# Conditioning rows of a fused state-space and SwiGLU block: four of six computed in four column parts of the matrix engine, the branch gate multiplied into K's column sums, a new order of loads and tasks

## The chip, the cores and the metric

The kernel runs on one core of one Trainium2 chip. A core has five instruction queues: PE (TensorE, matrix products), DVE (VectorE), ACT (ScalarE), POOL (GpSimd) and SP (SyncE, which here only issues transfers). Each queue takes its instructions strictly in program order; an instruction that waits for another engine or for a transfer holds those behind it. The metric is the device time of one launch in microseconds. Before the change it is 489.13 us, the median of 3 runs (488.37 to 490.04).

## The reference, cut to what matters

L = 2048 tokens, D = 448 channels, N = 256 states, F = 1792 hidden features, all in float32.

```python
mod = (silu(c) @ w_mod).reshape(1, 6, 1, D)      # c: 1 x 448, w_mod: 448 x 2688
sa, ca, ga, sb, cb, gb = mod[:, 0], ..., mod[:, 5]
h = layernorm(x) * (1 + ca) + sa
x = x + ga * (causal_conv(h, K) + h * Dskip)     # K from A, B, C, log_dt: 448 x 2048
h = layernorm(x) * (1 + cb) + sb
x = x + gb * ((silu(h @ w_gate) * (h @ w_up)) @ w_down)
```

The rows are numbered as in w_mod: 0 is the shift sa, 1 the scale ca, 2 the branch gate ga, 3 the shift sb, 4 the scale cb, 5 the gate gb of the end.

## The kernel before

The 2048 tokens are 16 tiles of 128, taken in blocks of 2, 2, 3, 3, 3 and 3 tiles. For each block a loop runs over 14 feature tiles f of 128 hidden features: `gate_up(f)` (L686) makes the gate and up products on PE with weights split into a rounded high and a low part, ScalarE takes the Silu, VectorE multiplies, ScalarE rounds the product (phi) and VectorE takes the low part (plo), and `down(f - 1)` (L739) adds the product of the feature tile before into one bank per token tile. Between these, the convolution part of the next block's tiles is done in steps.

Two paths exist for the convolution. A flag, computed on the chip from the size of dt * A, picks the short one with these inputs: K(l) is taken as m0 + l * m1 for every channel, so the convolution becomes products with a triangular matrix of ones (`tri`), a ramp and a running row (`run0`, `run1`) carried from tile to tile. m0 and m1 are sums over the states: `total` (L345, on ScalarE) and `slope` (L382, on VectorE). They come as columns (channels on partitions, four chunks of 128, the last with 64 channels twice) and are turned into a row, the same on all partitions, by `row_of` (L350): a matmul per chunk with the identity.

The change lies in the first 40 us, before block 0's feature loop. That stretch prepares everything: it loads x, the six state matrices (`sa` to `sf`, 448 KB each), w_mod's six groups (two loads each, 448 and 336 KB) and the first weights; computes the six rows, m0 and m1; does the convolution part of token tiles 0 and 1; normalises them, turns them to channels on partitions (`to_channels`) and splits them into high and low parts (`high`, `low`). Block 0's first feature tiles need the split weights w0, w1, w2 (`split_w`: ScalarE rounds, another engine takes the low part) and d0, d1 (`split_d`).

The order is written out by hand in two strings. `ORDER` (L41) gives SyncE's first loads. `PLAN` (L43) names tasks of the dictionary `todo`; each task issues its instructions on its engine when its name comes, so PLAN sets the order on every queue. Names: `pa`, `ps`, `pg`, `cb`, `sb` and `e` are the two halves of a row (1, 0, 2, 4, 3, 5); `S1` to `S3`, `a2`, `a3` the state sums; `k0`, `k1` the sums as rows; `o..` the products of tiles 0 and 1; `l0`, `l1` the left-over sums of these tiles for `run0` and `run1`, `lc` their copies; `tr`, `hi`, `lo` the turn to channels and the split; `x0`, `x1` the copies of the tiles out of their banks.

A row is computed by `mod_part` (L233): silu(c) as a stationary operand, repeated over 128 columns, against w_mod, so that the row comes out the same on all 128 partitions:

```python
pe.matmul(ps[:, 0:D], cs[:, k:k + 1].to_broadcast([128, 128]), w[:, k * D:(k + 1) * D],
          start=k == 0, stop=False)
```

Chunks 0 to 2 are summed in the bank; chunk 3 comes as two matmuls of 224 columns. The gate ga multiplies k0 and k1 as rows in their banks (`gm0`, `gm1` on VectorE) and the row of Dskip (`gd` on GpSimd), which was spread by a matmul at the start. The shift sb is added as a row after the normalisation (`norm_2`), and its columns `sbc`, for later blocks, come from four transposes (`cols`). The end gate is copied from its bank (`eg`) to `gb`, which is first used when block 0 ends (L808).

The flag is read into registers on every engine (L486) and a branch follows; then block 0 starts with gate_up(0), whose first bank is DN[2], and whose first instruction on ScalarE is the Silu (L718).

Of the kernel before, what the change touches and what calls it, by code (L numbers as in the profile page):

```python
# [40 lines left out]
ORDER = """sf x0 x1 sc m10 se m11 sd m20 m21 m00 sb m01 sa m40 m41 d0 w0 m30 m31 m50 w2 d1 x2 w1 x3 d2 m51"""  # L41

PLAN = """t1 t4 pa0 t2 pa1 pg0 pg1 t3 S1 ca h00 S2 ps0 wr wi ps1 a2 m0 t5 a3 sq1 k0 cb0 S3 ga cb1 w0 h01 gd h11 m1 k1 gm0 h10  # L43
hd0 sb0 gm1 hd1 gc1 v00 v10 gc0 o00 o01 sq0 o02 o10 v01 sa w02 d10 o13 st0 r0 o12 cbr v11 d11 o11 o14 sb1 n10 w2 w01
st1 r1 d00 sbr e0 n11 n20 du0 tr0 n21 hi0 du1 tr1 l0 fs l1 sbt lo00 hi1 w1 lo10 fl lo01 sbc x1 e1 lo11 w11 w21 x0 eg
w22 lc w12 d01"""
# [11 lines left out]
def tile_kernel(ctx, tc, x, a_re, a_im, b_re, b_im, c_re, c_im, log_dt, dskip,  # L58
# [172 lines left out]
    cs = const.tile([128, 5], F32)  # L231

# [11 lines left out]
    def end_gate(ks):  # L244

        mod_part(CV, m5.rearrange("p a b -> p (a b)"), ks)
# [9 lines left out]
    with tc.tile_pool(name="pre", bufs=1) as pre:  # L256
        vec = pre.tile([128, 8], F32)
        sc.dma_start(vec, vecs)
        drow = pre.tile([1, D], F32)
        sc.dma_start(drow, dskip.rearrange("(o d) -> o d", o=1))  # L260
# [36 lines left out]
        ve.memset(cs, 0.0)  # L297

# [25 lines left out]
        pe.matmul(pd, all1[0:1, :], drow, start=True, stop=True)  # L324
        sc.copy(gd, pd)
# [11 lines left out]
                               (("h", F32, D), ("v0", F32, D), ("v1", F32R, D), ("hd", F32, D), ("h2", F32, 512)))  # L337
        sbr = pre.tile([128, 512], F32)
        ga = pre.tile([128, D], F32)
        t_, WV = f32(tri), po  # L340
# [4 lines left out]
        def total(o, t, scale):  # L345
            for k in range(4):
                a = part(t, k)
                sc.activation(sca[:, 0:a.shape[1]], a, AF.Copy, scale=scale[:, k:k + 1], accum_out=o[:, k:k + 1])

        def row_of(m, ps):  # L350

            for k in range(4):
                n = 128 if k < 3 else 64
                pe.matmul(ps[:, k * 128:k * 128 + n], m[:, k:k + 1].to_broadcast([128, 128]), ident if k < 3 else ident2,
                          start=True, stop=True)
            return ps[:, 0:D]
# [9 lines left out]
        def row_sbuf(to, g, bias, ends=((0, 0, D),)):  # L366
            for a, o, n in ends:
                sc.activation(to[:, o:o + n], psm[g][:, a:a + n], AF.Identity, bias=bias)

        def cols():  # L370
            psm["c"] = bank()
            for k in range(4):
                pe.transpose(psm["c"][:, k * 128:(k + 1) * 128], sbr[:, k * 128:(k + 1) * 128], ident)

        def cols_sbuf():
            sc.copy(sbc, psm["c"].rearrange("p (k c) -> p k c", k=4)[:, :, 0])

        def gate_row():
            sc.copy(ga, psm[2][:, 0:D])  # L379
            sc.dma_start(gad, ga[0:1])  # L380
# [7 lines left out]
        def left_over(ks):  # L388
            if 0 in ks:
                psm["l"] = bank()  # L390
            for k in ks:
                u, w = ((f32(left[:, 0]), v0[k]) if k < 2 else (left[:, k - 1], v1[k - 2]))
                pe.matmul(psm["l"][0:33, 0:D], u, w, start=k == 0, stop=k == 3)  # L393

        def left_sbuf():
            for z, r in enumerate((run0, run1)):
                sc.copy(r[0:1], psm["l"][32 * z:32 * z + 1, 0:D])

        def to_channels(q):
            for k in range(4):  # L400
                if q == 0:
                    pk[k] = bank()
                pe.transpose(pk[k][:, q * 128:q * 128 + 128], h2[q][:, k * 128:(k + 1) * 128], ident)

        def high(q):
            for k in range(4):
                c_ = slice(q * 128, (q + 1) * 128)
                sc.copy(hhi[:, k, c_], pk[k][:, c_])

        def low(q, ks):  # L410
            for k in ks:
                c_ = slice(q * 128, (q + 1) * 128)
                ve.tensor_tensor(hlo[:, k, c_], pk[k][:, c_], f32(hhi[:, k, c_]), op=OP.subtract)

        def norm_1(q):
            ve.scalar_tensor_tensor(h2[q][:, 0:D], os[q], n2.of[q][0], cbw, op0=OP.subtract, op1=OP.mult)

        def norm_2(q):
            ve.scalar_tensor_tensor(h2[q][:, 0:D], h2[q][:, 0:D], n2.of[q][1], sbr[:, 0:D], op0=OP.mult, op1=OP.add)
# [4 lines left out]
        def flag_sum():  # L424
            psm["z"] = bank()
            pe.matmul(psm["z"][0:1, 0:2], ones, sz, start=True, stop=True)

        def flag_of():
            zm = pre.tile([1, 1], F32)
            ve.tensor_reduce(zm, psm["z"][0:1, 0:2], axis=AX.X, op=OP.add)  # L430
            ve.tensor_scalar(flag, zm, SMALL * SMALL, None, op0=OP.is_le)

        pk = {}
# [10 lines left out]
            "S1": do(total, m0_, t1, dt), "S2": do(total, m0, t2, ndt), "S3": do(total, a1, t4, dt2),  # L444
            "a2": do(slope, (0, 1)), "a3": do(slope, (2, 3)),
            "m0": add(m0, m0, m0_), "m1": add(m1, a1, a2), "k0": do(row_of, m0, CV), "k1": do(row_of, m1, DN[2]),

            **{f"{n}{z}": do(row, g, z) for n, g in (("pa", 1), ("ps", 0), ("pg", 2), ("cb", 4), ("sb", 3)) for z in range(2)},
            "ca": lambda: sc.activation(ca1, psm[1][:, 0:D], AF.Identity, bias=1.0),
            "sa": copy(sa, lambda: psm[0][:, 0:D]), "ga": gate_row,  # L450
# [593 lines left out]
```

## Time and profile before

| | |
|---|---|
| three runs | 488.37, 489.13, 490.04 us |
| the profiled execution | 488.68 us, its span 486.9 us |
| mean granted clock of PE | 0.998 |
| busy: PE, weight loads, VectorE, ScalarE, GpSimd | 98%, 92%, 58%, 32%, 13% |
| moved | 31.24 MB, mean 64 GB/s; 310, 415 and 161 GB/s in the first three fortieths (12.2 us each) |
| first matmul of block 0 | 38.64 us |

The span runs from the first to the last instruction; the execution has 1.8 us around it. In the profile a line of the timeline gives a group of like instructions: the start in us, the time from its first start to its last end, the engine (PEld is PE's weight load, ACTq and SPq are transfers being issued), the kernel's line, what is written and read, and the count; in brackets the idle time of that engine just before and what ended it. An f32 matmul shows as two records on PE. Ends of matmuls are modelled and overlap the next start, so the pace is read from the starts.

### The profile page before, as it was taken

The page shows a single profiled execution, that of the slowest core. Times are in us where ns is not written, and L with a number is a line of the kernel's source. Part 1 is how long each engine was busy: PE and PEld are TensorE (multiplying, and loading weights), DVE is VectorE, ACT ScalarE, POOL GpSimd, SP SyncE. Part 2 cuts the span into 40 slices and gives each one's busy share as a digit, 9 for nine tenths or more (in the row PEclk, how much of TensorE's full clock was granted, in tenths as well). Part 3 has the DMA queues.
Part 4 walks back from the last instruction along what each step waited for, and adds up shares of the span by engine and source line. Part 5 has one row for each costly group of instructions (what it writes and reads, how often), then busy time and mean ns, then how long its engine had stood idle before and what let it go on. Part 6 is the DMA issues. An engine that isn't in the chain of part 4 may idle for free.

```text
span 486.9 us, 6980 instructions
## 1 busy us (share of the span) xinstructions
PE 477.3 (98%) x2725; PEld 447.4 (92%) x2725; DVE 283.2 (58%) x543; ACT 155.0 (32%) x338; POOL 61.8 (13%) x86
## 2 busy tenths in 40 slices
PE   8999999999999999999999999999999999999994
PEld 5749988999998999999999999999999999999994
DVE  4868999568886446574644667375475643222134
ACT  5665455522225112332312223231223222221111
POOL 2241001000000040410023221002241000000000
PEclk9999999999999999999999999999999999999999
DMA  8945762020000200101210011130001112000001
GB/s 310 415 161 156 235 193 88 15 96 1 0 3 14 83 1 0 42 30 52 80 44 0 2 43 45 43 114 0 2 0 45 43 44 75 23 1 0 1 0 63
DMA packets 18751, 31.24 MB, mean 64 GB/s; under 512 B 2578, under 2 KB 13460, under 8 KB 18708
## 3 DMA queue, kind: packets, MB, share of 16 engines
q1 hardware_dynamic: 18000, 30.52, 18.3%
q8 instruction: 23, 0.38, 0.3%
q10 hardware_dynamic: 708, 0.19, 0.2%
q14 instruction: 20, 0.16, 0.1%
HBM read 24.61 MB, written 6.03 MB: 63 GB/s over the span
## 4 chain that ended last, share of the span: by engine, by line
PE 94%; DVE 2%; ACT 2%; issue 1%; POOL 0%; DVEq 0%; POOLq 0%; ACTq 0%
PE bank L703 57%; PE dn L747 27%; PE bank L237 2%; PE bank L253 1%; PE dn L437 1%; PE bank L241 1%; ACT raw L196 1%; PE bank L907 1%; PE cv L908 1%; PE cv L906 1%; PE cv L237 0%; PE bank L393 0%; DVE raw L194 0%; PE bank L207 0%; PE bank L920 0%
## 5 line engine op out<-in xcount | busy, mean ns | idle before, releaser
L703 PE MATMUL bank<-hhi,gu 128*128 128x384 f32 (+1 forms) x1169 | 209.4, 318 | 0.0
L703 PEld LDWEIGHTS bank<-hhi,gu 128*128 128x128 f32 x1169 | 189.8, 188 | 3.2 <-issue 0.7
L703 PE MATMUL bank<-hlo,gu 128*128 128x384 f32 (+1 forms) x668 | 130.8, 317 | 0.0
L703 PEld LDWEIGHTS bank<-hlo,gu 128*128 128x128 f32 x668 | 109.2, 188 | 0.0
L731 DVE TENSOR_TENSOR bank<-raw,bank 128x384 f32<-128x384 f32 (+1 forms) x69 | 36.8, 534 | 122.7 <-PE bank L703 120.3
L734 ACT CAST phi<-bank 128x384 fp32r<-128x384 f32 (+1 forms) x83 | 36.9, 445 | 140.8 <-DVE bank L731 140.8
L718 ACT ACTIVATE raw<-bank 128x384 f32<-128x384 f32 (+1 forms) x70 | 32.9, 470 | 121.8 <-PE bank L703 115.3
L735 DVE TENSOR_TENSOR plo<-bank,phi 128x384 fp32r<-128x384 f32 (+1 forms) x83 | 42.5, 512 | 37.6 <-ACT phi L734 37.6
L747 PE MATMUL dn<-wdh,plo 128*128 128x448 f32 x218 | 58.0, 367 | 0.0
L747 PE MATMUL dn<-wdh,phi 128*128 128x448 f32 x218 | 58.0, 367 | 0.0
L747 PE MATMUL dn<-wdl,phi 128*128 128x448 f32 x218 | 57.6, 365 | 0.0
L747 PEld LDWEIGHTS dn<-wdh,plo 128*128 128x128 f32 x218 | 41.0, 188 | 3.6
L747 PEld LDWEIGHTS dn<-wdl,phi 128*128 128x128 f32 x218 | 41.0, 188 | 3.5
L747 PEld LDWEIGHTS dn<-wdh,phi 128*128 128x128 f32 x218 | 38.7, 188 | 1.8 <-ACT run L930 0.7
L168 POOL TENSOR_SCALAR rsb<-mvb 128x1 f32<-128x1 f32 (+2 forms) x13 | 4.7, 360 | 170.6 <-DVE mvb L152 170.6
L168 POOL TENSOR_SCALAR rsa<-mva 128x3 f32<-128x3 f32 (+1 forms) x6 | 1.4, 233 | 118.1 <-DVE mva L152 118.1
L124 ACT CAST gu<-raw 128x1024 fp32r<-128x1024 f32 x14 | 14.6, 1046 | 0.3 <-ACT ga L379 0.3
L881 POOL TENSOR_TENSOR m<-m,gm 128x448 f32<-128x448 f32 x9 | 10.4, 1152 | 21.3 <-DVE m L185 21.3
L895 DVE TENSOR_TENSOR vl<-m,vh 128x448 fp32r<-128x448 f32 x12 | 9.1, 755 | 6.7 <-ACT vh L894 6.1
L237 PE MATMUL bank<-wm,cs 128*128 128x448 f32 x30 | 12.5, 546 | 0.0
L126 DVE TENSOR_TENSOR gu<-raw,gu 128x768 fp32r<-128x768 f32 x13 | 12.3, 950 | 0.0
L118 DVE TENSOR_TENSOR wdl<-rawd,wdh 128x448 fp32r<-128x448 f32 x16 | 9.9, 621 | 3.4 <-ACT wdh L116 3.2
(213 smaller groups left out, 417.8 us busy)
## 6 DMA issues: line engine op xcount, KB each, us to landing
raw<-in_B_w_gate_up_dram SPq DMA_DIRECT2D x14, 512.0 KB, 3.8
rawd<-in_B_w_down_dram SPq DMA_DIRECT2D x16, 224.0 KB, 3.9
x<-in_A_u_dram SPq DMA_DIRECT2D x12, 224.0 KB, 2.9
out_dram<-x SPq DMA_DIRECT2D x11, 224.0 KB, 2.4
xd<-raw SPq DMA_DIRECT2D x9, 256.0 KB, 2.0
raw<-xd SPq DMA_DIRECT2D x36, 64.0 KB, 2.0
wm<-in_w_mod_groups_dram SPq DMA_DIRECT2D x5, 448.0 KB, 8.0
wm<-in_w_mod_groups_dram SPq DMA_DIRECT2D x5, 336.0 KB, 7.9
```

What stands on the lines that cost most here:

```text
L118: ve.tensor_tensor(lo, wdn[j], f32(hi), op=OP.subtract)
L124: sc.copy(wgu[j][:, :, 0:4, :], w)
L126: en.tensor_tensor(lo, w[:, :, 0:3, :], f32(hi), op=OP.subtract)
L237: pe.matmul(ps[:, 0:D], cs[:, k:k + 1].to_broadcast([128, 128]), w[:, k * D:(k + 1) * D], start=k == 0, stop=False)
L703: pe.matmul(ps[s][:, 0:n], w[:, s, a], (hlo if lo else hhi)[:, k, 0:n], start=first and q == 0, stop=end and q == len(ka) - 1)
L718: sc.activation(p[:, 0:n], ps[0][:, 0:n], AF.Silu)
L731: ve.tensor_tensor(ps[1][:, 0:n], p[:, 0:n], ps[1][:, 0:n], op=OP.mult)
L734: sc.copy(hi[:, 0:n], ps[1][:, 0:n])
L735: ve.tensor_tensor(lo[:, 0:n], ps[1][:, 0:n], f32(hi[:, 0:n]), op=OP.subtract)
L747: pe.matmul(dn[q][:, 0:D], u[:, cs], v, start=f == 0 and z == 0, stop=f == (NF - 3 if last else NF - 1) and z == 2)
L881: (ve if on_v else po).tensor_tensor(v, h, g, op=OP.mult)
L895: ve.tensor_tensor(vl, v0, f32(vh), op=OP.subtract)
```

## The change

Rows 2, 3, 4 and 5 are computed by a new function, `mod_quads`: each chunk k of 128 channels has its own 32 columns of the array and its own 32 partitions of the bank, so that four partial sums of the row stand in partitions 0, 32, 64 and 96. ScalarE copies the bank (`gpc`, `cpc`, `spc`, `gqc`). A vector `pick` with ones in partitions 0, 32, 64 and 96 then adds the four: for rows 2, 3 and 5 with the copy as stationary operand, which gives the sum as columns (`columns`: `gt`, `sbt`, `gbt`; five matmuls of one moving column each), for row 4 with `pick` as stationary operand, which gives it as a row (`ck`).

The gate ga, now as columns `gac`, multiplies m0, m1 and Dskip while these are columns of 4 elements; `gm0` and `gm1` fall away. Dskip comes with the small first load and is turned into a row by four matmuls (`gdr`). The shift sb is not added after the normalisation but with the split: `high` adds `sbc` on ScalarE, `low` on VectorE, with two chunks in one bank. The end gate goes as columns to DRAM and from there, repeated on all partitions, into `gb`; ScalarE issues these three transfers. The left-over sum for `run0` takes v0 of both tiles, added by GpSimd (`v0s`). w0's low part moves from GpSimd to VectorE. ORDER and PLAN are new: w_mod's groups come ahead of most weights.

```diff
-ORDER = """sf x0 x1 sc m10 se m11 sd m20 m21 m00 sb m01 sa m40 m41 d0 w0 m30 m31 m50 w2 d1 x2 w1 x3 d2 m51"""
+ORDER = """sf x0 x1 sc m10 se sd m11 m20 m21 m00 sb m01 sa m40 m41 m30 m31 w0 m50 m51 d0 w1 d1 x2 w2 x3 d2"""
...
-st1 r1 d00 sbr e0 n11 n20 du0 tr0 n21 hi0 du1 tr1 l0 fs l1 sbt lo00 hi1 w1 lo10 fl lo01 sbc x1 e1 lo11 w11 w21 x0 eg
+w01 spc v0s gq w02 fs tr0 sbt xn1 fl sbc gqc hi0 l0 lo0 tr1 l1 hi1 gbt lo1 gbc x0 x1 w1 d00 w11 w12 lc d01 w2 w21 w22 d10 d11"""
...
-    def end_gate(ks):
-
-        mod_part(CV, m5.rearrange("p a b -> p (a b)"), ks)
+    def mod_quads(ps, w):
+
+        for k in range(3):
+            pe.matmul(ps[32 * k:32 * k + 32, 0:D], cs[:, k:k + 1].to_broadcast([128, 32]), w[:, k * D:(k + 1) * D],
+                      start=True, stop=True)
+        for z in range(2):
+            pe.matmul(ps[96:128, z * D // 2:(z + 1) * D // 2], cs[:, 3 + z:4 + z].to_broadcast([128, 32]), w[:, 3 * D:NM],
+                      start=z == 0, stop=z == 1)
+
+    def chunks(t, k):
+
+        if k < 3:
+            return [(slice(0, 128), t[:, k * 128:(k + 1) * 128])]
+        return [(slice(64 * z, 64 * z + 64), t[:, 384:D]) for z in range(2)]
+
+    def to_dram(row, col):
+
+        sc.dma_start(row[:, 0:384].rearrange("o (k p) -> p (o k)", p=128), col[:, 0:3])
+        sc.dma_start(row[:, 384:D].rearrange("o p -> p o"), col[0:64, 3:4])
...
-        pd = bank()[:, 0:D]
-        pe.matmul(pd, all1[0:1, :], drow, start=True, stop=True)
-        sc.copy(gd, pd)
...
-        t_, WV = f32(tri), po
+        t_, WV = f32(tri), ve
...
+        def columns(n):
+
+            for k in range(4):
+                for e, t in chunks(qt[n], k):
+                    pe.matmul(psm[n][e, 448 + k:449 + k], t, pick, start=True, stop=True)
+
+        def spread_row():
+            pe.matmul(psm["c"][:, 0:D], pick.to_broadcast([128, 128]), qt["c"], start=True, stop=True)
+
+        def gd_row():
+            psm["d"] = bank()
+            row_of(gdm, psm["d"], ident[:, 0:64])
+
+        def end_gate():
+            sc.copy(gbc, psm["b"][:, 448:452])
+            to_dram(gbd, gbc)
+            sc.dma_start(gb, gbd.to_broadcast([128, D]))
+
+        def scaled(o, a, b):
+            po.tensor_tensor(o, a, b, op=OP.add)
+            po.tensor_tensor(o, o, gac, op=OP.mult)
+
+        def slope_of():
+            ve.tensor_tensor(m1, a1, a2, op=OP.add)
+            ve.tensor_tensor(m1, m1, gac, op=OP.mult)
...
-        def left_over(ks):
-            if 0 in ks:
-                psm["l"] = bank()
-            for k in ks:
-                u, w = ((f32(left[:, 0]), v0[k]) if k < 2 else (left[:, k - 1], v1[k - 2]))
-                pe.matmul(psm["l"][0:33, 0:D], u, w, start=k == 0, stop=k == 3)
+        def left_over(z):
+            if z:
+                for k in range(2):
+                    pe.matmul(CV[0:33, 0:D], left[:, 1 + k], v1[k], start=False, stop=k == 1)
+            else:
+                pe.matmul(CV[0:33, 0:D], f32(left[:, 0]), v0s, start=True, stop=False)
...
                 if q == 0:
-                    pk[k] = bank()
-                pe.transpose(pk[k][:, q * 128:q * 128 + 128], h2[q][:, k * 128:(k + 1) * 128], ident)
+                    pk[k] = pk[k - 1][:, 256:512] if k % 2 else bank()
+                o = pk[k][:, q * 128:q * 128 + 128]
+                if k < 3:
+                    pe.transpose(o, h2[q][:, k * 128:(k + 1) * 128], ident)
+                else:
+                    for e, t in chunks(h2[q], k):
+                        pe.matmul(o[e], t, ident, start=True, stop=True)
...
-                sc.copy(hhi[:, k, c_], pk[k][:, c_])
+                sc.activation(hhi[:, k, c_], pk[k][:, c_], AF.Identity, bias=sbc[:, k:k + 1])
...
         def flag_sum():
-            psm["z"] = bank()
-            pe.matmul(psm["z"][0:1, 0:2], ones, sz, start=True, stop=True)
+            pe.matmul(psm["s"][0:1, 460:462], ones, sz, start=True, stop=True)
```

How the queues change at the places that matter: first ScalarE's queue at the end of the stretch, before. The names: `hhi` is the rounded high part, `gu_158` is w1, `cv` holds the end gate's row, `dn_68` and `dn_69` are the banks of tiles 0 and 1, `p` is the Silu of gate_up(0).

```order
L408 CAST hhi<-bank 128x128 [waits PE_49] x2
L124 CAST gu_158<-raw 128x2x512 [waits DMAHW3_49]
L376 COPY sbc<-bank 128x4 [waits PE_49]
L473 COPY x_73<-dn_69 128x448 [waits DMAHW4_49]
L473 COPY x_72<-dn_68 128x448
L438 COPY gb<-cv 128x448 [waits PE_49]
L397 COPY run<-bank 1x448 x2
L486 TENSOR_LOAD flag [waits DVE_49]
L975 COMPARE_AND_BRANCH
L718 ACTIVATE p<-dn_70 128x256 [waits PE_49]
```

And after the change, from the end gate's columns `gbc` on; here w1 is `gu_154`, w2 `gu_160`, and `wdh_151` and `wdh_156` are d0 and d1:

```order
L400 COPY gbc<-bank 128x4 [waits PE_49]
L263 DMA gbd<-gbc 128x3x1 [waits DMAHW5_49,Activation_49]
L264 DMA gbd<-gbc 64x1 [waits DMAHW6_49]
L402 DMA gb<-gbd 128x448 [waits DMAHW7_49,DMAHW6_49,DMAHW5_49]
L509 COPY x_72<-dn_68 128x448 [waits DMAHW2_49]
L509 COPY x_73<-dn_69 128x448
L123 CAST gu_154<-raw 128x2x512
L115 CAST wdh_151<-rawd_81 128x448
L427 COPY run<-cv 1x448 x2
L123 CAST gu_160<-raw 128x2x512 [waits DMAHW2_49]
L115 CAST wdh_156<-rawd_82 128x448 [waits DMAHW0_49]
L755 ACTIVATE p<-dn_70 128x256 [waits PE_49]
```

The roundings of w1, d0, w2 and d1 have moved from before and between the high parts to behind them, and three transfers stand ahead of all of these; the third waits for the first two (DMAHW5 and DMAHW6).

Second, PE's queue from the first transposes to the flag, before (`h_0` and `h_1` are the normalised tiles, `sz` the flag's sums, `m_79` w_mod's group 5):

```order
L403 MATMUL bank<-ident,h_0_257 128x128 [waits DVE_49]
L403 MATMUL bank<-ident,h_0_257 128x128 [waits PE_49,Activation_49] x3
L403 MATMUL bank<-ident,h_1_258 128x128 [waits DVE_49,Activation_49]
L403 MATMUL bank<-ident,h_1_258 128x128 [waits Activation_49] x3
L393 MATMUL bank<-v_0_251,left 33x448 [waits DVE_49]
L393 MATMUL bank<-v_1_252,left 33x448
L426 MATMUL bank<-sz,ones 1x2 [waits DVE_49]
L393 MATMUL bank<-v_0_253,left 33x448
L393 MATMUL bank<-v_1_254,left 33x448
L373 MATMUL bank<-ident,sbr 128x128 [waits DVE_49]
L373 MATMUL bank<-ident,sbr 128x128 x3
L237 MATMUL cv<-m_79,cs 128x448 [waits DMAHW6_49]
```

And after it (`qts` is the copy of row 3, `t_240` is v0 of both tiles):

```order
L458 MATMUL bank<-sz,ones 1x2 [waits Activation_49]
L435 MATMUL bank<-ident,h_0_260 128x128 x2
L435 MATMUL bank<-ident,h_0_260 128x128 [waits PE_49]
L438 MATMUL bank<-ident,h_0_260 64x128 x2
L390 MATMUL bank<-pick,qts 128x1 x3
L390 MATMUL bank<-pick,qts 64x1 x2
L423 MATMUL cv<-t_240,left 33x448 [waits Pool_49]
L435 MATMUL bank<-ident,h_1_261 128x128 [waits DVE_49,Activation_49]
L435 MATMUL bank<-ident,h_1_261 128x128
L435 MATMUL bank<-ident,h_1_261 128x128 [waits DVE_49]
L438 MATMUL bank<-ident,h_1_261 64x128 x2
L421 MATMUL cv<-v_0_256,left 33x448
```

The second tile's transposes, which followed the first's with a wait for ScalarE, now stand behind the shift's columns and one left-over product, and wait for VectorE (the low parts of the first tile, which read the same banks); the matmuls of the end gate's row are gone from this place (its four-part row stands ahead of it, its columns behind).

More of the change, by code (lines that the diff above doesn't have):

```diff
@@ L231, in tile_kernel @@
     cs = const.tile([128, 5], F32)
+    pick = const.tile([128, 1], F32)
+    gac = const.tile([128, 4], F32)
+    gbd = dram.tile([1, D], F32, name="gbd")
     def mod_part(ps, w, ks):
@@ L297, in tile_kernel @@
         ve.memset(cs, 0.0)
+        ve.memset(pick, 0.0)
+        for q in range(4):
+            ve.memset(pick[32 * q:32 * q + 1], 1.0)
         left = pre.tile([128, 3, 33], F32R)
@@ L364, in row, with quads @@
             mod_part(psm[g], wms[g], (0, 1) if z == 0 else (2, 3))
[L366 to L371, printed above, removed]
-            for k in range(4):
[L373 to L380, printed above, removed]
+        def quads(n, g):
+            psm[n] = bank()
+            mod_quads(psm[n], wms[g])
+        def columns(n):
+            for k in range(4):
+                for e, t in chunks(qt[n], k):
[15 more added lines that the diff above has]
+            ve.tensor_tensor(m1, m1, gac, op=OP.mult)
         def slope(ks):
@@ L448, in tile_kernel @@
[L448 to L453 removed]
+            "m0": do(scaled, m0, m0, m0_), "m1": slope_of, "k0": do(row_of, m0, CV), "k1": do(row_of, m1, DN[2]),
```

77 lines of the change are left out of this document (39 added, 38 removed).

## The prediction

> **What bounds the kernel now.** I read the page first, its busy shares and the chain that ended last:
>
> ```profile
> PE 477.3 (98%) x2725; PEld 447.4 (92%) x2725; DVE 283.2 (58%) x543; ACT 155.0 (32%) x338; POOL 61.8 (13%) x86
> PE 94%; DVE 2%; ACT 2%; issue 1%; POOL 0%; DVEq 0%; POOLq 0%; ACTq 0%
> ```
>
> TensorE (PE) carries 94% of the chain and idles nowhere for long. So whatever shifts the moment at which PE reaches the feed-forward blocks shifts the end, and a delay inside block 0 isn't won back: no later wait is left for it to vanish into. The change lies wholly ahead of that, so I went to the timeline of PE over the first 50 us (start, duration, line):
>
> ```profile
> 8.81 1.01 PE L324 MATMUL bank<-drow,all 1*128 1x448 f32 x2
> 9.75 2.52 PE L237 MATMUL bank<-wm,cs 128*128 128x448 f32 x6
> 12.87 2.42 PE L237 MATMUL bank<-wm,cs 128*128 128x448 f32 x6
> 15.12 0.92 PE L241 MATMUL bank<-wm,cs 128*128 128x224 f32 x4
> 15.88 2.42 PE L237 MATMUL bank<-wm,cs 128*128 128x448 f32 x6
> 18.89 1.00 PE L354 MATMUL cv<-ident,m 128*128 128x128 f32 x8
> 19.73 2.47 PE L237 MATMUL bank<-wm,cs 128*128 128x448 f32 x6
> 25.19 0.92 PE L437 MATMUL dn<-v,tri 128*128 128x448 f32 x2
> 25.94 0.92 PE L437 MATMUL dn<-hd,ident 128*128 128x448 f32 x2
> 38.64 0.44 PE L703 MATMUL dn<-hhi,gu 128*128 128x256 f32 x1
> 41.31 0.96 PE L703 MATMUL bank<-hhi,gu 128*128 128x256 f32 x7
> 43.81 0.57 PE L747 MATMUL dn<-wdh,phi 128*128 128x448 f32 x2
> 44.22 0.57 PE L747 MATMUL dn<-wdl,phi 128*128 128x448 f32 x2
> 45.04 0.97 PE L703 MATMUL bank<-hhi,gu 128*128 128x256 f32 x7
> ```
>
> Durations overlap, so prices are differences of starts. A modulation row is 12.87 to 15.88, 3.0 us, in eight records' worth of 0.375; an f32 matmul of 448 columns 0.75 (25.19 to 25.94); a rounded one 0.2 (two in 43.81 to 44.22); a column turned into a row (L354, eight records) 0.84 (18.89 to 19.73). Gate and up of the first feature tile, f0, start at 38.64, f1 at 41.31, the first down sum at 43.81, f2 at 45.04. I measure the change by where f2 starts.
>
> Transfers come next: two stretches of the windows (last columns: DMA share, GB/s), landings from the DMA list, issues from SyncE's timeline.
>
> ```profile
> 10.00:14.00 4.00, 4.00 (x14) 2.33 (x14) 3.95 (x5) 3.62 (x12) 0.00 (x0) 1.00 1.03 418
> 30.00:34.00 4.00, 3.97 (x18) 2.34 (x16) 2.83 (x7) 1.82 (x8) 1.95 (x3) 1.00 0.01 2
> se<-in_A_states_dram SPq DMA_DIRECT2D x1, 448.0 KB, 6.3
> sa<-in_A_states_dram SPq DMA_DIRECT2D x1, 448.0 KB, 8.1
> 3.05 0.43 SPq L266 DMA_DIRECT2D se<-in_A_states_dram  x1
> 9.41 0.33 SPq L266 DMA_DIRECT2D sa<-in_A_states_dram  x1
> ```
>
> The 16 DMA engines are full, at 418 GB/s, until about 30 us. A 448 KB load takes 458,752 B / 418 GB/s = 1.1 us of it; se lands at 3.05 + 6.3 = 9.35, sa at 9.41 + 8.1 = 17.5. PE and the transfers are both nearly full up to 30 us; neither can run far ahead of the other.
>
> **The change, PE up to f0.** Unknown is the price Q of a four-part row. No matmul of before writes a narrow column part, so its ends are 3.0 (no overlap) and 0.75 (four at once: two records of 0.375). I take 1.9. An f32 matmul leaves two records on the same columns of the array, which can't overlap each other, and PE runs matmuls in order; so the second record of one part runs beside the first of the next: five steps of 0.375. The measured rows give no nearer price. The Trainium skill ("TensorE: Matmul & The Clock Gate", Part 3, measured speedup) states 2.38 times for three column parts at once; by it Q would be 3.0 / 2.38 = 1.26, an estimate, and the sum 2.2 us lower. No run here shows it.
>
> A set of columns (five matmuls of one moving column, ten records with weight loads) I take at 1.05, by L354's 0.105 a record; ends 0.85 and 1.6.
>
> PE's new order, end to end: the skip row's broadcast is gone, so row 1 starts at 8.8; its second half needs m11, now behind sd: 9.35 + 1.1 + 0.8 = 11.2, so 0.9 is waited and it ends at 12.7. Gate row 2 in four parts, to 14.6; half of row 0, to 16.1; the gate's columns, to 17.2 (ScalarE copied the bank by 15.4); the other half, 18.7; k0, 19.5; the new gd row, 20.3; o00 and o10, 21.8. k1 stood behind ScalarE's sums:
>
> ```profile
> 18.62 0.51 ACT L348 ACTIVATE sca<-t,dt 128x256 f32<-128x256 f32 x1 [1.56 <-DVE t L435]
> 21.05 0.16 DVE L436 TENSOR_TENSOR m<-a,a 128x4 f32<-128x4 f32 x1 [0.25 <-ACT sca L348]
> ```
>
> These start once sa has landed and been multiplied, in the new order too, so m1 is there at 21.5, two small VectorE steps instead of one. k1 runs 21.8 to 22.7, o01 to 23.4, row 4 to 25.3, five more products and the spread of row 4 to 28.1, rows 3 and 5 to 31.9, flag and first transposes to 32.9, the shift's columns to 34.0, one left-over to 34.7. Here PE waits. The shift's columns share a bank with the flag's sum, so the flag on VectorE (two steps like L436's, 0.35), then on ScalarE sbc (four columns, 0.25 as an estimate) and the copy of row 5 (half of L473's 0.97 below), then the roundings, come one after the other; and as two chunks now share a bank, the second tile's transposes stand behind VectorE's low parts of the first:
>
> ```profile
> 33.03 0.77 ACT L408 CAST hhi<-bank 128x128 fp32r<-128x128 f32 x4
> 33.71 1.11 DVE L413 TENSOR_TENSOR hlo<-bank,hhi 128x128 fp32r<-128x128 f32 x4 [0.51 <-PE bank L403]
> ```
>
> With 0.3 for the first rounding and 1.2 for the four low parts the transposes start at 36.6, take 0.85, and the last left-overs and the gate's columns end at 38.9. That is f0: 38.9 against 38.64, +0.2. At Q = 0.75 the same list gives 35.5, at 3.0 43.3.
>
> What the change removes is thus mostly spent again: four rows at 1.1 less each, and 0.75 each for the skip broadcast and a left-over sum, against three column sets, the gd row, the spread row and some 2.7 us of waits.
>
> **The change, f0 to f2.** The end gate now goes through DRAM from ScalarE's queue. Behind these three DMAs ScalarE holds both x copies, the rounding of w1 (PE's f1 needs it), d0, the run rows, w2, d1, and only then f0's Silu. Before, the roundings lay ahead of f0, in ScalarE's waits for PE. ScalarE does hold while an issue waits:
>
> ```profile
> 69.53 0.53 ACT L930 COPY run<-bank 32x448 f32<-32x448 f32 x1 [1.89 <-PE bank L920]
> 71.02 0.61 ACTq L932 DMA_DIRECT2D run<-run  x1
> 71.67 0.57 ACT L116 CAST wdh<-rawd 128x448 fp32r<-128x448 f32 x1 [1.62 <-DVE x L933]
> run<-run ACTq DMA_DIRECT2D x13, 3.5 KB, 1.7
> xd<-raw SPq DMA_DIRECT2D x9, 256.0 KB, 2.0
> ```
>
> L116 had its input and stood 1.62 us behind a DMA whose data came late. The landings, 1.7 and 2.0, bound the small writes; I take 2.0, the row that writes DRAM, and up to 3.0 since every element is a piece of its own. Issues take 0.33 (sa) to 0.61 (L932); I take 0.4. The other prices:
>
> ```profile
> 37.55 0.97 ACT L473 COPY x<-dn 128x448 f32<-128x448 f32 x2
> 34.71 1.07 ACT L124 CAST gu<-raw 128x1024 fp32r<-128x1024 f32 x1
> 39.44 1.05 ACT L397 COPY run<-bank 1x448 f32<-1x448 f32 x2
> 37.57 1.81 DVE L126 TENSOR_TENSOR gu<-raw,gu 128x768 fp32r<-128x768 f32 x2
> 41.12 0.39 ACT L718 ACTIVATE p<-dn 128x256 f32<-128x256 f32 x1 [0.63 <-PE dn L703]
> 41.61 0.43 DVE L731 TENSOR_TENSOR bank<-p,bank 128x256 f32<-128x256 f32 x1 [0.80 <-ACT p L718]
> ```
>
> Column copy done 39.1; first write issued to 39.5; the second lands at 41.5; load of gb issued to 41.9; x copies to 42.8; w1 rounded 43.9, its low part on VectorE (1.0) 44.9. So PE, done with f0 at 41.5, runs all but f1's first matmul from 44.9 to 47.3. ScalarE meanwhile does d0, run rows, w2, d1 (0.5 + 1.0 + 0.95 + 0.5) to 46.6, then the Silu; VectorE has the low parts of w2 and d1 ahead of the product, which starts at 48.1; its rounding is done at 48.9, the down sum starts, and f2 at 50.2. Before, 45.04: **+5.1 us**. Of it 0.2 are ahead of f0 and 4.9 between f0 and f2 (11.3 against 6.4). The rest I cost at nothing. gb is first used when block 0 ends. w0's low part on VectorE instead of GpSimd ends at 31.8, and GpSimd's sum for the left-overs at 31.9, both ahead of PE's need at 34 to 39. On SyncE's queue the load of w4 waits for w1's staging buffer, free at 45.3:
>
> ```profile
> raw<-in_B_w_gate_up_dram SPq DMA_DIRECT2D x14, 512.0 KB, 3.8
> ```
>
> It lands at 49.1; ScalarE rounds it behind f2's Silu, after 52. Were that cover gone, PE would wait for it at f4.
>
> The profiled execution took 488.68, so 493.8; the median of the three runs, 489.13, lies 0.45 above, so 494.2.
>
> **The rivals.** A is the forecast, parts in pairs.
>
> B: more parts overlap. For it: the parts share no columns. Q = 0.75 puts f0 at 35.5 and f2 at 46.8, +1.7 us, 490.8; with short landings and columns at 0.85, +0.7, 489.9. The Trainium skill's 2.38 ("TensorE: Matmul & The Clock Gate", Part 3) lies in this case.
>
> C: no overlap, the rows still cost 3.0. For it: no row here shows one. f0 at 43.3, +9.5 us, 498.6. This is also the case in which the change doesn't do what it says.
>
> D: A, and PE's clock drops in the new gap. The array ran slowly after standing:
>
> ```profile
> 1.58 5.79 PE L253 MATMUL bank<-tri 128*128 128x512 f32 x14 [1.58 <-DVE tri L286]
> ```
>
> These are 0.41 each, where 448 columns later take 0.2, though the granted-clock column reads 1.00. PE does one matmul from 41.5 to 44.9. Another 5.8 us at half rate would cost 2.9, of which 1.5 fall into the wait for the product: +1.4 on top of A, 495.6. The Trainium skill ("TensorE: Matmul & The Clock Gate", Part 1) puts the fall after an idle window of about 3.4 us; a gap of 3.4 cut by one matmul is at the edge of that, and the slow start above agrees with it.
>
> E, faster: the three DMAs hold ScalarE for nothing, the parts overlapping fully. The place is ahead of the x copies, the price 2.8 us less. It decides from f0 before 35.5 on, 3.1 ahead, if f0 to f2 takes less than 9.5. Then f2 is at 44.0, 1.1 ahead; with columns at 0.85, 43.5: 487.6. Against it: L116 above.
>
> **How the numbers follow.** A 0.42, B 0.25, C 0.14, D 0.10, E 0.09. The likeliest gives 494.2. The range runs from B's low end, 489.9, to C with a little more landing, 499.0; E and the tails are left out. 0.3% is 1.5 us, about what a measurement can tell. Faster by more: 0.07 from E. Within: 0.02 from E and 0.06 from B's low end, 0.08. Slower: 0.85.
>
> **What would show it.** The starts of the four-part matmuls: one row's eight records in 1.9 (A), about 0.75 (B), 3.0 (C). f0 at 38.9. ScalarE idle for about 1.6 us ahead of the issue of gb, w1 rounded near 43.9, f1 broken off after one matmul, the first Silu about 5 us after f0's end, f2 at 50.2. Wrong would be the forecast if f1 followed f0 without a gap, or if f0 came before 35.

## The result, and the profile after

The changed kernel takes 504.25 us (median of 4 runs, 503.44 to 505.79), the kernel before 488.84 in the same session; the ratio is 1.0315 (95% interval 1.0284 to 1.0347). It is slower, as forecast, but by 15 us instead of 5: 5 us outside the range. The profiled execution took 504.15, its span is 502.1 against 486.9, so 15.2 us are to be found.

Of the changed kernel: the chain that ended last, the issues in the DMA list (KB, us to landing), and its windows (PE, PEld, DVE, ACT, POOL busy, granted clock, DMA share, GB/s):

```profile
PE 88%; DMA 5%; DVE 3%; ACT 3%; issue 1%; ACTq 0%; SPq 0%; DVEq 0%
```

```profile
gbd<-gbc ACTq DMA_DIRECT2D x1, 1.5 KB, 11.0
gbd<-gbc ACTq DMA_DIRECT2D x1, 0.2 KB, 11.1
```

```profile
30.00:36.00 6.00, 4.40 (x30) 2.53 (x31) 4.17 (x11) 3.23 (x11) 2.12 (x2) 1.00 0.20 43
36.00:42.00 6.00, 6.00 (x33) 5.96 (x32) 0.86 (x3) 0.49 (x3) 0.00 (x0) 0.52 0.17 52
42.00:51.00 9.00, 0.35 (x2) 0.05 (x1) 0.00 (x0) 1.48 (x3) 0.00 (x0) 0.69 0.05 15
51.00:58.00 7.00, 6.10 (x28) 5.73 (x29) 5.71 (x10) 5.22 (x10) 0.00 (x0) 0.59 0.51 136
```

PE's share of the chain fell from 94% to 88% and DMA has 5% of it. From the end of f0 at 42.3 to the x copies at 49.5 nothing computes: everything waits for two small writes that land after 11 us. Nor is anything moved: from 39.5 to 49.0 the busy share of the DMA engines is 0.00. Their records of the 448 pieces end at 39.4, the landing is reported at 49.1. The granted clock is about a half from 36 to 42 and again around 51 to 58.

PE's timeline (row 3 and the first half of row 5, the second tile's transposes, f0, f1, first down sum, f2), then ScalarE's (ACT):

```profile
28.20 0.57 PE L249 MATMUL bank<-wm,cs 128*32 128x448 f32 x3
28.22 0.56 PE L252 MATMUL bank<-wm,cs 128*32 128x224 f32 x2
...
28.97 0.55 PE L249 MATMUL bank<-m,cs 128*32 128x448 f32 x3
...
34.53 0.76 PE L435 MATMUL bank<-ident,h 128*128 128x128 f32 x3 [1.41 <-DVE hlo L448]
...
37.29 0.58 PE L740 MATMUL dn<-hhi,gu 128*128 128x256 f32 x1
...
51.49 0.58 PE L740 MATMUL bank<-hhi,gu 128*128 128x256 f32 x1 [9.14 <-ACT gu L123]
52.48 1.65 PE L740 MATMUL bank<-hhi,gu 128*128 128x256 f32 x6 [0.41 <-DVE gu L125]
...
56.96 0.57 PE L784 MATMUL dn<-wdh,phi 128*128 128x448 f32 x2
...
58.18 0.99 PE L740 MATMUL bank<-hhi,gu 128*128 128x256 f32 x7
```

```profile
37.41 0.16 ACT L400 COPY gbc<-bank 128x4 f32<-128x4 f32 x1 [1.08 <-PE bank L390]
37.60 0.39 ACTq L263 DMA_DIRECT2D gbd<-gbc  x1
38.02 0.52 ACTq L264 DMA_DIRECT2D gbd<-gbc  x1
49.15 0.34 ACTq L402 DMA_DIRECT2D gb<-gbd  x1
49.52 0.97 ACT L509 COPY x<-dn 128x448 f32<-128x448 f32 x2 [11.96 <-DMA gbd<-gbc]
50.38 1.06 ACT L123 CAST gu<-raw 128x1024 fp32r<-128x1024 f32 x1
...
54.28 0.38 ACT L755 ACTIVATE p<-dn 128x256 f32<-128x256 f32 x1
```

Up to f0 the change wins 1.35 us (37.29 against 38.64). From f0 to f2 it loses 14.5 (20.9 against 6.4). From f2 to the last gate and up it loses 2.3 more (429.8 against 427.5), and the tail gives 0.25 back: 15.2. The last loss is a slower pace; two neighbouring feature tiles of block 1, before and after:

```profile
104.94 0.97 PE L703 MATMUL bank<-hhi,gu 128*128 128x256 f32 x7
...
108.67 0.97 PE L703 MATMUL bank<-hhi,gu 128*128 128x256 f32 x7
```

```profile
119.22 1.00 PE L740 MATMUL bank<-hhi,gu 128*128 128x256 f32 x7
...
123.06 0.99 PE L740 MATMUL bank<-hhi,gu 128*128 128x256 f32 x7
```

3.73 us from tile to tile became 3.84, at a granted clock of 1.00. The three-tile blocks go at 5.7 in both.

### The profile page after: what moved, and what is told of

It is laid out like the page before. It is cut to its first block, busy times and chain, and to the rows that moved or that the text cites. A ratio compares the mean times of both kernels' runs of the same rounds, so it can differ in the third digit from the quotient of the medians.

```text
span 502.1 us, 7070 instructions
## 1 busy us (share of the span) xinstructions
PE 480.2 (96%) x2763; PEld 452.1 (90%) x2763; DVE 284.2 (57%) x546; ACT 156.5 (31%) x340; POOL 60.6 (12%) x87
## 4 chain that ended last, share of the span: by engine, by line
PE 88%; DMA 5%; DVE 3%; ACT 3%; issue 1%; ACTq 0%; SPq 0%; DVEq 0%
PE bank L740 56%; PE dn L784 26%; DMA gbd<-gbc 2%; DMA wm<-in_w_mod_groups_dram 2%; DMA x<-in_A_u_dram 1%; ACT raw L195 1%; PE bank L239 1%; PE dn L469 0%; PE bank L944 0%; PE cv L943 0%; DVE gu L125 0%; PE cv L945 0%; ACT gu L123 0%; DVE raw L193 0%; PE bank L390 0%
## 5 line engine op out<-in xcount | busy, mean ns | idle before, releaser
L740 PE MATMUL bank<-hhi,gu 128*128 128x384 f32 (+1 forms) x1169 | 214.2, 322 | 9.6 <-ACT gu L123 9.1
L740 PEld LDWEIGHTS bank<-hhi,gu 128*128 128x128 f32 x1169 | 193.5, 190 | 13.2 <-ACT gu L123 9.4
L740 PE MATMUL bank<-hlo,gu 128*128 128x384 f32 (+1 forms) x668 | 133.0, 321 | 0.0
L740 PEld LDWEIGHTS bank<-hlo,gu 128*128 128x128 f32 x668 | 111.4, 190 | 0.0
L123 ACT CAST gu<-raw 128x1024 fp32r<-128x1024 f32 x14 | 14.6, 1046 | 0.0
L937 POOL TENSOR_TENSOR m<-m,gd 128x448 f32<-128x448 f32 x9 | 11.5, 1283 | 0.0
```

What stands on the lines that cost most here:

```text
L123: sc.copy(wgu[j][:, :, 0:4, :], w)
L740: pe.matmul(ps[s][:, 0:n], w[:, s, a], (hlo if lo else hhi)[:, k, 0:n], start=first and q == 0, stop=end and q == len(ka) - 1)
L937: (ve if on_v else po).tensor_tensor(h, h, gd, op=OP.mult)
```

## The experiments

Sixteen kernels ran; they are numbered as they ran. "Time" is the median, with the ratio to the kernel before in the same session (488.3 to 489.2 us). The theory: ScalarE stands 12 us behind a landing that the many 4-byte pieces make long, and the two new tiles, which push the weights 64 bytes on, set the pace.

**1. The end gate by TensorE.** Base: the changed kernel.

```diff
-            sc.copy(gbc, psm["b"][:, 448:452])
-            to_dram(gbd, gbc)
-            sc.dma_start(gb, gbd.to_broadcast([128, D]))
+            sc.copy(gb, psm["b"][:, 0:D])
-            "gbt": do(columns, "b"), ...
+            "gbt": do(spread_row, "b"), ...
```

> The end gate's row 5 is spread over the partitions by one TensorE matmul and copied to gb, so its three DMAs are gone; the rest is the changed kernel. Theory (ScalarE's 12 us hold behind the DMAs is the loss): ScalarE has no gap after 37.5, w1 is rounded by about 40, f1 follows f0 within 1 us, f2 starts at 45.5 to 47.5 instead of 58.2, time 491.5 to 493.5. Rival (the order of ScalarE's tasks is the loss, the roundings now behind f0): f2 at 50 or later, time above 496.

491.69 us, ratio 1.0046 (1.0029 to 1.0064); f0 to f2 is 9.8 us instead of 20.9. Two rows of ScalarE's timeline and two of PE's:

```profile
38.52 0.53 ACT L400 COPY gb<-bank 128x448 f32<-128x448 f32 x1 [1.74 <-PE bank L393]
...
39.80 1.07 ACT L123 CAST gu<-raw 128x1024 fp32r<-128x1024 f32 x1
```

```profile
41.92 0.99 PE L738 MATMUL bank<-hhi,gu 128*128 128x256 f32 x6 [0.51 <-DVE gu L125]
...
47.43 0.99 PE L738 MATMUL bank<-hhi,gu 128*128 128x256 f32 x7
```

The gap is gone, and with it 12.6 of the 15.4 us: the three DMAs were most of the loss, in both ways, by the hold and by the half rate that followed it.

**2. The same DMAs on GpSimd.** `to_dram` and the load of gb are issued by `po` instead of `sc`.

> The same three DMAs, issued from GpSimd's queue. Theory (the landing of many 4-byte pieces in DRAM is long by itself, and only whoever waits for it loses): landings stay near 11 us, GpSimd stands in ScalarE's place, f2 at 46 to 48, time 492 to 494. Rival (the long landing comes from ScalarE's queue or from what is around it): landings of 2 to 3 us on GpSimd. Rival (the landing also delays other things): time above 498.

494.42 us, ratio 1.0118 (1.0077 to 1.0159). DMA list, then GpSimd (POOL) and ScalarE:

```profile
gbd<-gbc POOLq DMA_DIRECT2D x1, 1.5 KB, 11.6
gbd<-gbc POOLq DMA_DIRECT2D x1, 0.2 KB, 10.7
```

```profile
49.73 0.59 POOL L402 DMA_DIRECT2D gb<-gbd  x1 [10.72 <-DMA gbd<-gbc]
```

```profile
49.40 1.04 ACT L123 CAST gu<-raw 128x1024 fp32r<-128x1024 f32 x1 [5.02 <-DMA gbd<-gbc]
```

The landing is as long on another queue, and f2 starts at 46.1. But ScalarE still meets it: the rounding of w3, the first into memory that the stage ahead frees, has both writes among its waits, and stands 5.0 us. So a hold taken off one queue came back, smaller, through the reuse of memory. The run costs 2.7 us more than run 1.

Nor is it only the one who waits that loses, as the theory here had it. This is the time to landing of the loads of gate and up weights issued from 30 to 56 us:

```profile
DMA to landing us min/median/max: 3.7/4.7/11.8
```

The one issued at 33.64 landed after 3.7, those issued at 40.45 and 42.77, while the writes were under way, after 11.0 and 11.8, and a load of 224 KB issued at 43.21 after 12.0. In run 1, without the writes, the three issued from 42.40 to 45.17 took 3.6 to 4.1. The rounding of w4 starts at 51.48, just after its load has landed at 51.46.

**3. The row in one piece.** Run 1's spread, then one partition of it to DRAM (1.75 KB) and back, both on ScalarE:

```diff
+            sc.copy(qt["b"][0:1], psm["b"][0:1, 0:D])
+            sc.dma_start(gbd, qt["b"][0:1])
+            sc.dma_start(gb, gbd.to_broadcast([128, D]))
```

> Row 5 spread by TensorE as in the first run; one partition of it (1.75 KB, one piece) goes to DRAM and back to all partitions, both DMAs on ScalarE. Theory (pieces of 4 bytes make the landing long): the write lands in about 2 us, ScalarE stands 1.5 to 2 us, f2 at 48 to 50, time 494 to 496.5. Rival (any write from ScalarE here lands late): landing near 11 us, time 502 to 504.

493.58 us, ratio 1.0094 (1.0063 to 1.0124), a little under the expected time; f2 starts at 48.7. ScalarE:

```profile
38.66 0.49 ACTq L401 DMA_DIRECT2D gbd<-qtb  x1
39.83 0.35 ACTq L402 DMA_DIRECT2D gb<-gbd  x1
40.22 0.97 ACT L509 COPY x<-dn 128x448 f32<-128x448 f32 x2 [1.59 <-DMA gbd<-qtb]
```

It stands 1.59 us in all, 0.84 of it the two issues. The load of gb, which waits for the write, is issued 1.17 after the write. Queue, place and size are those of the changed kernel. What differs is the number of pieces, and with it the source (one partition instead of 128) and the number of writes (one instead of two); run 7 has the same source in both patterns.

**7. Landings by themselves.** The kernel before with eight small writes from SyncE in blocks 2 to 5, each pair issued together.

> The kernel before, with eight small writes into DRAM from SyncE in quiet stretches of blocks 2 to 5: 384 pieces of 4 bytes side by side, 64 of them, one row of 1792 bytes, 384 pieces of 4 bytes 64 bytes apart, 384 of them 512 bytes apart, 128 of 16 bytes, 128 of 64 bytes, 16 of 4 bytes. Theory (every piece below a certain size costs the same, the count sets the landing): 384 pieces 10 to 11 us wherever they lie, 128 pieces 4 to 5, 64 pieces 3 to 4, 16 pieces and the row 2. Rival (neighbours in the same few bytes of DRAM wait for each other): the spaced ones 2 to 4 us, the 64 side by side near 10. Rival (the stretch of the program made it long): all 2 to 3.

The trace has the landings of five. In the order of issue: 384 pieces side by side, 64 side by side right behind them, 384 that lie 64 bytes apart, 128 of 16 bytes, 16 of 4 bytes side by side; those of the row, of the 384 that lie 512 bytes apart and of the 128 of 64 bytes are missing:

```profile
pr<-sbc SPq DMA_DIRECT2D x1, 1.5 KB, 7.6
pr<-sbc SPq DMA_DIRECT2D x1, 0.2 KB, 7.3
pr<-sbc SPq DMA_DIRECT2D x1, 1.5 KB, 2.5
pr<-sbc SPq DMA_DIRECT2D x1, 2.0 KB, 2.6
pr<-sbc SPq DMA_DIRECT2D x1, 0.1 KB, 2.1
```

The count alone isn't it: 384 pieces land after 2.5 us when they lie 64 bytes apart, after 7.6 side by side. My theory of the count falls. Lying side by side alone isn't it either: 16 such pieces land after 2.1. (The 64 stand right behind the 384, so their 7.3 is no price of their own.) The time passes after the pieces have been sent: the last of the DMA engines' records of the 384 ends 2.3 us after the issue when they lie side by side and 2.0 when they lie 64 bytes apart, and the landing follows 5.4 and 0.5 later. That pieces in the same few bytes of DRAM wait for each other fits this, but is not shown. All of it is one profiled execution, and why the same pattern takes 10.2 to 11.6 in the place of the end gate stays open.

**4. The pace: 64 bytes.** The kernel before and an unused tile:

```diff
     cs = const.tile([128, 5], F32)
+    pad = const.tile([128, 16], F32, name="pad")
+    ve.memset(pad, 0.0)
```

> The kernel before with one unused 64-byte tile ahead of the weights, which moves all weight tiles by 64 bytes as the change's two new tiles do. Theory (the place of the weights in SBUF sets the pace of 256-column matmuls): blocks 0 and 1 go at 0.1185 us a matmul instead of 0.1135, 0.1 us more for each feature tile, time 490.4 to 491.0. Rival (the pace comes from something else in the change): 0.1135 as before, time 488.4 to 489.3.

491.52 us, ratio 1.0046 (1.0028 to 1.0064), with 3.84 us a feature tile in blocks 0 and 1. An unused tile costs this kernel 2.6 us.

**8. All tiles 64 bytes on** (the same pad ahead of every tile).

> The kernel before with 64 unused bytes ahead of all its tiles, so that the weights and the moving operand hhi both lie 64 bytes further on. Theory (the weights' own address sets the pace): 0.1185 us a matmul as in the fourth run, profiled span near 490. Rival (the distance between weights and moving operand sets it): 0.1135, span near 487 to 488.

One run: span 487.5; block 1 at 3.75, as before. So it is not the weights' own address. Block 0 went at 3.82 here, but also in run 7, where nothing was moved.

**5. 128 bytes instead of 64** (run 1 and the pad).

> The first run's kernel with 64 unused bytes more ahead of the weights, so that they lie 128 bytes further on than before instead of 64. Theory (the slow pace goes with the address modulo 128): 256-column matmuls at 0.1135 us again, f2 still near 47.4, time 2.2 to 2.6 below the first run, 489.1 to 489.5. Rival (any move of the weights slows them): 491.7.

487.64 us, ratio 0.9970 (0.9956 to 0.9984). Faster than expected, and for another reason: two-tile blocks at 3.82, but the three-tile blocks at 5.63 instead of 5.70. The address modulo 128 is not the rule.

**6. The roundings ahead** (run 5's kernel, the list of tasks).

```diff
-... n11 w01 spc v0s gq w02 fs tr0 sbt xn1 fl sbc gqc hi0 l0 lo0 tr1 l1 hi1 gbt lo1 gbc x0 x1 w1 d00 w11 w12 lc d01 w2 w21 w22 d10 d11
+... n11 w01 spc v0s w02 fs tr0 sbt xn1 w1 fl sbc hi0 l0 gq lo0 gqc w11 tr1 l1 hi1 gbt lo1 w2 gbc x0 x1 w12 lc d00 d01 w21 w22 d10 d11
```

> The kernel of the run above, and in the list of tasks w1's rounding, its first low part, w2's rounding and the copy of row 5 are moved ahead into ScalarE's and VectorE's waits for TensorE, and row 5's matmuls behind the first left-over, where TensorE waits 1.4 us. Theory (what is left between f0 and f2 is ScalarE's late roundings and the half rate after that wait): f1 follows f0 without a gap, f0 runs at 0.113 us a matmul, f2 at 43.3 to 44.5, time 487.0 to 488.5, at or below the kernel before. Rival (VectorE's low parts are the bound there anyway): f2 at 46 or later, time 489 to 490.

486.16 us, ratio 0.9945 (0.9923 to 0.9966): below the kernel before. f1 follows f0 without a gap, but f2 starts at 45.4, later than expected, as VectorE's low parts end only at 43.2. The second tile's transposes on PE and the same window (PE busy, granted clock, DMA), of run 5:

```profile
34.88 0.81 PE L435 MATMUL bank<-ident,h 128*128 128x128 f32 x3 [1.41 <-DVE hlo L448]
```

```profile
36.00:38.00 2.00, 2.00 (x9) 0.50 0.42 162
```

and of this run:

```profile
35.27 0.75 PE L435 MATMUL bank<-ident,h 128*128 128x128 f32 x3 [0.22 <-DVE hlo L448]
```

```profile
36.00:38.00 2.00, 2.00 (x14) 1.00 0.71 246
```

With row 5's matmuls in the wait of 1.4 us, the clock stayed full; as ScalarE's tasks were moved too, this run does not tell which of the two did it.

**14. The x copies ahead too.**

```diff
-... cbw n10 sp st1 xn0 r1 n11 ... sbt xn1 w1 fl ... lo1 w2 gbc x0 x1 w12 lc d00 d01 w21 w22 d10 d11
+... cbw x0 n10 sp st1 xn0 r1 n11 ... sbt x1 xn1 w1 fl ... lo1 w2 gbc w12 w21 w22 d00 d10 d01 d11 lc
```

> The kernel with the roundings ahead (distance 448); the two x copies also moved into ScalarE's waits ahead of the second norm steps, w2's low parts ahead of d0's and d1's on VectorE, the run rows last. Theory (ScalarE's remaining tasks ahead of the first Silu are what f2 waits for): Silu at 40.3 instead of 41.2, the product at 40.9 instead of 43.2, the down sum follows f1 without a gap, f2 at 43.7 to 44.2 instead of 45.4, time 484.4 to 485.0. Rival (the copies delay the norm steps): f0 later by up to 1, time 486.

484.44 us, ratio 0.9922 (0.9902 to 0.9943), the best of all. ScalarE's first Silu, then PE's flag sum, first down sum and f2:

```profile
40.16 0.39 ACT L755 ACTIVATE p<-dn 128x256 f32<-128x256 f32 x1
```

```profile
29.80 0.19 PE L458 MATMUL bank<-sz,ones 128*1 128x2 f32 x2 [1.29 <-ACT qts L484]
...
42.51 0.58 PE L784 MATMUL dn<-wdh,phi 128*128 128x448 f32 x2
...
43.74 0.99 PE L740 MATMUL bank<-hhi,gu 128*128 128x256 f32 x7
```

f2 comes 1.3 us earlier than in the kernel before, with no wait left between f0 and f2. The clock was low here from 32 to 35.5 (0.58 and 0.57 in its windows): PE had waited 1.29 us for the copy of row 3, which now stands behind an x copy, with small matmuls behind the wait. Run 15, the same but for 32 bytes, kept full rate.

**12. Whole rows.** Run 6 with rows 2, 4, 3 and 5 over all 128 columns.

```diff
-            mod_quads(psm[n], wms[g])
+            mod_part(psm[n], wms[g], range(4))
```

> The kernel with the roundings ahead (distance 448), rows 2, 4, 3 and 5 as whole rows again, one after the other over all 128 columns, and the column sums read from one partition. Theory (four column parts run at once, 0.76 us instead of 3.0 a row): TensorE has up to 9.0 us more ahead of f0, less what its waits there take up (some 2.5): f0 at 43.5 to 46 instead of 37.15, time 6 to 9 above that kernel, 492.2 to 495.2. Rival (the transfers bound the stretch, the narrow parts win little): f0 below 41, time below 490.

492.49 us, ratio 1.0070 (1.0047 to 1.0094), 6.3 more than run 6. PE has row 3 and f0:

```profile
31.78 2.42 PE L241 MATMUL bank<-wm,cs 128*128 128x448 f32 x6
...
43.04 0.61 PE L739 MATMUL dn<-hhi,gu 128*128 128x256 f32 x1
```

f0 is 5.9 us later than in run 6 (37.15), and against the kernel before, each in its own session, the two are 7.2 apart: the column parts are worth some 6 to 7 us.

**9 to 11. The distance between weights and moving operand.** The distance is the address of the gate and up weights in a partition less that of `hhi`, as the tiles are allocated. Tiles of `const` are put ahead of `hhi` instead of behind it, in run 6's kernel; this is run 9, and runs 10 and 11 move others:

```diff
+    pick = const.tile([128, 1], F32)
+    gac = const.tile([128, 4], F32)
     hhi = const.tile([128, 4, MB * 128], F32R)
...
-    pick = const.tile([128, 1], F32)
-    gac = const.tile([128, 4], F32)
```

> The kernel with the roundings ahead, the pad taken out and the two new tiles put ahead of the moving operand hhi, so that weights and hhi lie as far apart as before (320 bytes modulo 512; 384 in the changed kernel, 448 in the kernel with the roundings ahead). Theory (this distance sets the pace): block 1 at 3.73 us a feature tile instead of 3.82, the three-tile blocks at 5.70 instead of 5.63, so 1.0 to 2.3 us won and 3.6 lost: 487.3 to 488.8. Rival (the pace differs by chip or run, not by the distance): the paces and the time of the kernel with the roundings ahead, 486.2.

> The same, with gd and three small tiles also ahead of hhi: distance 0 modulo 512. Theory (distance sets the pace): a third pair of paces, different from both, in either direction; rival: 3.82 and 5.63 again.

> The same, with gd alone ahead of hhi: distance 128 modulo 512. Theory (distance sets the pace): paces of its own; if 64 bytes is the grain and 448 the best for three tiles, no better than 5.63 a feature tile; rival: 3.82 and 5.63 again.

487.56 (ratio 0.9979, 0.9960 to 0.9997), 488.27 and 489.51 us (one run each of the last two). In run 9 the three-tile blocks go back to 5.71 and block 0 to 3.73, run 10 has paces of its own, and run 11 those of distance 384: the unchanged paces of the rival came in none of them.

**13. The changed kernel with the distance of before** (the same two lines moved, nothing else).

> The changed kernel whole, its DMAs too, with the two new tiles put ahead of hhi, so that weights and hhi lie 320 bytes apart modulo 512 as before. Theory (2 of the 15 us come from that distance): 256-column feature tiles at 3.73 or 3.82 us instead of 3.835 to 3.847, time 0.8 to 2.3 below the changed kernel's 504.2, 501.9 to 503.4; the hold of 11 to 12 us on ScalarE stays. Rival (in this kernel the pace comes from the late start): pace and time unchanged.

501.42 us, ratio 1.0263 (1.0244 to 1.0282), 2.8 below the changed kernel. Its profile, of the fastest of the four executions (499.78), has a span 4.6 us shorter: 427.7 us from f2 to the last gate and up instead of 429.8, so 2.1 by the pace; 0.6 between f0 and f2, where the landing was shorter (10.2); 0.4 ahead of f0 and 1.5 in the tail, which one execution does not explain.

**15 and 16. Half steps**, in run 14's kernel.

> That kernel with weights and hhi 480 bytes apart modulo 512 instead of 448. Theory (the grain is 64 bytes): paces of distance 448, 3.82 and 5.63, or of distance 0, 3.85 and 5.67 to 5.69. Rival (32 bytes matter): other paces.

> That kernel with 416 bytes. Theory (the grain is 64 bytes): paces of distance 384, 3.84 and 5.70, or of distance 448, 3.82 and 5.63. Rival (32 bytes matter): other paces.

487.04 and 490.68 us, one run each. All of these together, as medians of the eleven start-to-start times from f2 to f13 on PE, one profiled execution of each kernel (us; runs without a pace of their own share a row):

| distance mod 512 | kernels | two tiles, block 0 | block 1 | three tiles |
|---|---|---|---|---|
| 0 | run 10 | 3.85 | 3.85 | 5.67 to 5.69 |
| 128 | run 11 | 3.84 | 3.85 | 5.69 to 5.70 |
| 320 | before; runs 7, 8 | 3.82 | 3.75 | 5.69 to 5.71 |
| 320 | runs 9, 13 | 3.73 | 3.82 | 5.71 |
| 384 | changed; runs 1 to 4 | 3.84 | 3.85 | 5.69 to 5.70 |
| 416 | run 16 | 3.88 | 3.88 | 5.71 to 5.73 |
| 448 | runs 5, 6, 12, 14 | 3.82 | 3.82 | 5.63 |
| 480 | run 15 | 3.80 | 3.80 | 5.67 to 5.71 |

The same distance gives the same pace in kernels that differ in much else, 128 and 384 agree, 32 bytes count. Only at 320 the pace changes within a block: in the kernel before, the first five steps of block 0 take 3.73 us and the last three 3.82 (in runs 7 and 8 all of these take 3.82), and in run 9 block 1 goes from 3.73 to 3.82 and back; what switches it stays open. That the pace goes with the distance is shown; by what mechanism is not, nor that 512 is the period: as 128 and 384 agree, 256 would fit as well.

## Why the prediction was wrong

The direction, the place (f0 to f2) and the mechanism, ScalarE standing behind its DMAs with the roundings behind it, were right. Three sizes were not, and the pace of the main loop stood in no step.

**The landing, "I take 2.0 ... and up to 3.0": it was 11.05.** This is the step that failed. Counted from f0's start, the second write landed at +2.6 in the forecast and at +11.8 on the chip; w1 was rounded at +5.0 and at +14.15, the first Silu began at +7.7 and at +17.0, f2 at +11.3 and at +20.9. The 9.2 us run through unchanged, and f1 at half rate (52.48 to 56.96, 4.5 us) adds 0.4. The row I took, xd, writes long pieces. In run 3, with one long piece, ScalarE stands 1.6 in all where I had summed 2.8 (39.1 to 41.9), or 2.4 with one write instead of two: there the step errs the other way. I had noted that every element is a piece of its own and gave 1 us for it, with no row that could show the price; that bound should have been left open far above. The Trainium skill ("DMA: Bandwidth & Descriptors", latency and other measured facts) gives a DMA about 2 us of fixed cost, most of it the round trip of the receipt from the memory. By that, too, the term would have come out at 2, an estimate; run 3's write took 1.2 at most and the one here 11.

**The four-part row, "I take 1.9": it was 0.77.** In the timeline the next row begins 0.77 us after 28.20, and the first records of the four parts start within 20 ns of each other. A part's second record does wait for its first (0.40 us); what fell is the premise that the records run in order part by part, so that the next part waits too: all first records run together, then all second ones. The term belonged to case B. The Trainium skill's 2.38 times ("TensorE: Matmul & The Clock Gate", Part 3) would have given 1.26, an estimate; here four parts gained 3.0 / 0.77 = 3.9 times.

**f0, "38.9", or "35.5" in case B: it was 37.29.** With rows of 0.77 it is case B's list that has to hold, and f0 came 1.8 later than it says. Some 1.3 of that stood already at row 3 (28.20 for 26.9, the list with Q = 0.75), 0.6 of it at k1 (22.41 for 21.8). Behind that, the list had PE's own matmuls up to the wait; the chain in order of time has other engines there:

```profile
26.69 0.94 ACT gu L123
...
30.26 0.87 DVE gu L125
31.14 0.96 DVE gu L127
...
32.44 0.16 DVE zm L462
...
32.62 0.16 ACT sbc L490
```

w0's rounding (L123) stands on ScalarE ahead of cbw, for which the norm step on VectorE waits. w0's low parts, which I costed at nothing as PE needs them late, stand on VectorE ahead of the flag, and sbc waits for the flag's bank. That they are needed late was not the question; what stands behind them was. The price of the low parts was small here, some 0.4 as an estimate: without them sbc would have waited for the shift's columns, which end at 32.03, and from there to the second tile's transposes (34.53) it took 2.5 us for a forecast of 2.6. Half rate then made the gate's columns 1.3 us (36.01 to 37.29) instead of 1.04 (30.99 to 32.03).

**The clock (rival D)** did fall, before the gap that I named: from 36.3 to 43.1, beginning 1.7 us after PE's 1.4 us wait for the low parts, and again from 46.5 to 56.7, around f1. On the path it cost little, as f0 ran inside ScalarE's hold. The Trainium skill ("TensorE: Matmul & The Clock Gate", Part 1) has the fall after an idle window of about 3.4 us; here the clock fell in runs 5 and 14 after waits of 1.3 to 1.4 us with small matmuls around them, and in run 15 not. A gap as long as the rule's was not needed.

**The pace** was in no step: 2.3 us for two tiles of 4 and 16 bytes a partition.

By the sum: +5.1 were forecast; f0 was 1.55 better than forecast, f0 to f2 9.6 worse, the pace and the tail added 2.05: 15.2. The point that a delay ahead of block 0 is not won back held. So did m11's wait (1.25 us for a forecast of 0.9) and the set of columns (1.04 for 1.05).

## What to carry to other kernels

A small write has no price of its own: look at how many pieces it has and whether they lie side by side in DRAM, and never put an in-order engine with work for the critical path behind its landing, nor loads that are needed soon (run 2); a row spread by one matmul cost less than any of the three ways through DRAM. When a tile is added between the operands of the main loop's matmuls, compare the pace of the main loop before and after, not only the place that was edited. A task that is needed late still has a price if something short stands behind it on its engine.

## What the hardware showed that I had not expected

- 448 pieces of 4 bytes side by side in DRAM landed after 10.2 to 11.6 us from ScalarE's and GpSimd's queues; 384 of them after 7.6, and after 2.5 when they lie 64 bytes apart. Loads issued while such a write was under way landed after 11.0 to 12.0 us, against 3.7 before it.
- A row's f32 matmuls in four column parts of 32 took 0.77 us together, a whole row 3.0.
- The pace of rounded matmuls goes with the distance in SBUF between weights and moving operand: 3.73 to 3.88 us a two-tile feature tile and 5.63 to 5.73 a three-tile one. Runs 14 and 16, which differ in 32 bytes of an unused tile, are 6.2 us apart, 1.3% of the kernel (one run of 16).
- The granted clock fell to a half after waits of 1.3 to 1.4 us between small matmuls, though not each time.
